# A fused attention and gated-convolution kernel: the last batch's gate products and the previous batch's output tiles move in between the last transform stages

## The chip, the cores and the metric

The kernel runs on one core of one Trainium2 chip. The metric is the device time of one execution in microseconds. The time before the change is the median of three runs.

## The reference

Two layers stand behind each other. The first is attention with a sparse mask (8 global keys and a causal window of 96 keys) and a bias by distance, over 4 batches, 8 heads, 768 positions and head size 64. The second is a gated long convolution over the sequence:

```python
x = attn_out.transpose(0, 2, 1, 3).reshape(B, S, H * D)     # (4, 768, 512)
proj = x @ w_proj                                            # (4, 768, 1536)
x1, x2, x3 = proj[..., :D], proj[..., D:2 * D], proj[..., 2 * D:]
X2 = np.fft.rfft(x2, n=S, axis=1)
Hf = np.fft.rfft(filter_fft, n=S, axis=0)[None]
x2_conv = np.fft.irfft(X2 * Hf, n=S, axis=1)
y = x1 * x2_conv * x3
out = y @ w_out                                              # (4, 768, 512)
```

The product `x1 * x3` is called the gate below, since it does not depend on the convolution.

## The kernel before, in words

The kernel does not issue its work as it is written down. Each method records operations in a `Plan`, with the keys that each reads and writes and a guessed cost. `Plan.schedule` then lists them greedily: of all operations that could start, it takes the one with the earliest start by its model, and among those within 0.03 us of each other the one with the smallest key. The key is the place of the operation's batch in time (`batch`, in periods of 40) plus `bias`. PSUM has 8 banks, each taken by one group of matmuls until it has been copied out, and the list scheduler hands them out. The result is a fixed order for each engine: TensorE (PE), VectorE (DVE), ScalarE (ACT), GpSimd (POOL) and the DMA queue of SyncE (SP). On the chip every engine works through its own list in order and waits where a semaphore tells it to.

Where the model leaves TensorE idle for long enough, `Plan.fill` writes extra matmuls on a tile of zeros into a spare bank (`busy`, line 356, tile `idle`). Their result is never read.

For each of four batches there are two parts, and the attention of batch b+1 is scheduled beside the convolution of batch b:

- `attention(b)`: transposes of q and k (line 608), scores (633), exp on ACT (645), masking on DVE (653, 656), values (677, 682), normalising on DVE (696, 697, tile `xn`), transposes of the result (712) into `xT`. This runs in three column groups c = 0, 1, 2. After c = 1 and c = 2 come the gates of one half of the sequence each: for each of four 128-column blocks j, `gate` runs two groups of four matmuls with 384 columns (739), scales the one by ACT into `x1` (364) and multiplies the other by it on DVE into `g` (747). At the end the butterfly makes `xa` and `xb` from the two sequence halves of `xT` (724, 726).
- `conv(b)`: six projection groups of four matmuls (line 783 before, 786 after) into `ab`; six forward transforms of three matmuls (595) into `X`; the products with the filter's spectrum on DVE (`spectra`, 852 to 863 before, 867 to 878 after); eight inverse transforms of three matmuls (803 before, 806 after) into `eo`; then on DVE the sum and the difference of `eo` give the two halves of `y` (812 before, 844 after), and each is multiplied by `g` (815 before, 847 after); last six output groups of four matmuls (826) are scaled by ACT into `ot` (364) and stored by a DMA of 256 KB from SP (834).

When the last batch's convolution begins, no attention is left to go beside it.

Of the kernel before, what the change touches and what calls it, by code (L numbers as in the profile page):

```python
# [29 lines left out]
def dve(n, rate=1, psum=False):  # L30
    return 0.068 + (0.005 if psum else 0.0) + n / rate / 960.0


def pe(*cols):
    return sum(n / 2400.0 + 0.0025 for n in cols)
# [242 lines left out]
class Fused:  # L278
# [472 lines left out]
    def attention(self, b):  # L751
        self.g.batch = (self.PERIOD * (b - 1 + self.SHIFT), self.PERIOD * self.LONG)
        for c in range(3):
            new = ([0, 1, 2], [3, 4], [5])[c]
            for t in new:
                self.transposes("q", t, self.qn[:, t], P * t)
            for t in self.GRP[c]:
                self.transposes("k", t, self.kn[:, t], P * t)
            for i in range(4):
                self.scores(i, c)  # L760
            for i in range(4):
                self.values(i, c, b % 2)
                if i % 2:
                    self.transpose_x(i // 2, c)
            if c:
                for j in range(4):
                    self.gate(b, j, c - 1)
        for j in range(2):
            self.butterfly(j)


    def conv(self, b):
        nc, g, DM, S = self.nc, self.g, self.DM, self.S
        h, last = S // 2, b == self.B - 1
        g.batch = (self.PERIOD * b, self.PERIOD)
        X, y, w = self.X, self.y, self.w
        for i, (src, key) in enumerate(((self.xa, "xa"), (self.xb, "xb"))):
            for t in range(3):
                bk = g.bank()

                def proj(_, src=src, t=t, bk=bk):
                    for c in range(4):
                        nc.tensor.matmul(bk.f32(), src[:, c, P * t:P * t + P], w[:, c, DM:2 * DM],  # L783
                                         start=(c == 0), stop=(c == 3))
                g.op("P", pe(*[512] * 4), proj, acq=[bk], r=[(key, 0), (key, 1)] + [
                    ("w", n) for n in range(4, 8)], name="proj")
                g.op("AV", self.evac(512), lambda e, i=i, t=t, bk=bk: self.copy(
                    e, self.ab[i][:, t, :], bk.f32()), use=[bk], w=[("ab", i, t)],
                    name="ab")
            if i == 0:  # L790
                self.spectra(b, (0, 1))
        self.spectra(b, (2, 3))
        self.spectra(b, (4, 5))
        for jp in range(2):
            eo, ke = self.eo[jp], ("eo", jp)
            for jj in range(2):
                for par, slots in ((0, (0, 1, 4)), (1, (2, 3, 5))):
                    bk = g.bank()
                    cs = slice(P * (2 * jp + jj), P * (2 * jp + jj) + P)

                    def turn(_, bk=bk, cs=cs, slots=slots):
                        for s in slots:
                            nc.tensor.matmul(bk.f32()[:, 0:h], X[:, s, cs], self.inv[:, s, :],  # L803
                                             start=(s == slots[0]), stop=(s == slots[-1]))
                    g.op("P", pe(h, h, h), turn, acq=[bk], r=[("X", s) for s in slots] + [("inv", s) for s in slots], name="inv")
                    g.op("AV", self.evac(h), lambda e, eo=eo, jj=jj, par=par, bk=bk: self.copy(
                        e, eo[:, jj, par], bk.f32()[:, 0:h]), use=[bk], w=[ke + (jj, par)], name="eo")
            yv = y[:, 2 * jp:2 * jp + 2].rearrange("p j (s n) -> p j s n", s=2)
            rs = [ke + (jj, par) for jj in range(2) for par in range(2)]
            gt = self.gt[b % 2]  # L810
            for half, fn in ((0, nc.vector.tensor_add), (1, nc.vector.tensor_sub)):
                g.op("V", dve(2 * h, 2), lambda _, fn=fn, yv=yv, eo=eo, half=half: fn(
                    yv[:, :, half], eo[:, :, 0], eo[:, :, 1]), r=rs, w=[("y", jp, half)], name="half")
                js = slice(2 * jp, 2 * jp + 2)
                g.op("V", dve(2 * h, 2), lambda _, js=js, half=half, gt=gt: nc.vector.tensor_mul(
                    y[:, js, h * half:h * half + h], y[:, js, h * half:h * half + h],
                    gt[:, js, h * half:h * half + h]),
                    r=[("y", jp, half)] + [("g", b % 2, j, half) for j in (2 * jp, 2 * jp + 1)],
                    w=[("y", jp, half)], name="y*g")
        osc = 1.0 / (S * H_SCALE * X1_SCALE)  # L820
        for t in range(6):
            bk = g.bank()

            def project(_, t=t, bk=bk):
                for c in range(4):
                    nc.tensor.matmul(bk.f32(), y[:, c, P * t:P * t + P], self.wo[:, c, :],  # L826
                                     start=(c == 0), stop=(c == 3))
            g.op("P", pe(*[512] * 4), project, acq=[bk], r=[("y", 0, t // 3), ("y", 1, t // 3), "wo"],
                 name="out")
            o = self.outs % 6  # L830
            self.outs += 1
            g.op("AV", self.evac(512), lambda e, o=o, bk=bk: self.times(e, self.ot[o], bk.f32(), osc),
                 use=[bk], w=[("ot", o)], name="ot")
            g.op("S", 0.5, lambda _, o=o, t=t, b=b: nc.sync.dma_start(
                self.out[b, P * t:P * t + P, :], self.ot[o]), r=[("ot", o)], nbytes=(128, 2048))

    def spectra(self, b, pair):
        nc, g, X = self.nc, self.g, self.X
        n = pair[0] // 2
        for s in pair:  # L840
            bk = g.bank()
            self.forward(s, self.ab, lambda i: [("ab", i, t) for t in range(3)], bk)
            g.op("AV", self.evac(512), lambda e, s=s, bk=bk: self.copy(e, X[:, s], bk.f32()),
                 use=[bk], w=[("X", s)], name="X")
        xs = X[:, pair[0]:pair[0] + 2]
        k = self.turn2 % 2
        self.turn2 += 1
        p1, p2 = self.p1[k], self.p2[k]
        hk = [("h", s) for s in pair] if n < 2 else [
            ("h", s, i, d) for s in pair for i in (1, 2) for d in (0, 64)]  # L850
        rs = [("X", s) for s in pair] + hk
        g.op("V", dve(1024, 2), lambda _: nc.vector.tensor_mul(p1, xs, self.h1[:, pair[0]:pair[0] + 2]),  # L852
             r=rs, w=[("p1", k)], name="prod")
        g.op("V", dve(1024, 2), lambda _: nc.vector.tensor_mul(p2, xs, self.h2[:, pair[0]:pair[0] + 2]),
             r=rs, w=[("p2", k)], name="prod")

        def sums(_):
            if n < 2:
                nc.vector.tensor_add(xs[:, 0], p1[:, 0], p2[:, 1])
                nc.vector.tensor_add(xs[:, 1], p1[:, 1], p2[:, 0])  # L860
            else:
                nc.vector.tensor_add(xs[0:64], p1[0:64], p2[64:P])
                nc.vector.tensor_add(xs[64:P], p1[64:P], p2[0:64])
        g.op("V", 2 * dve(512 if n < 2 else 1024, 2), sums, r=[("p1", k), ("p2", k)],
             w=[("X", s) for s in pair], name="sums")
# [96 lines left out]
```

## Time and profile before

| | |
|---|---|
| median of 3 runs | 207.98 us (206.68 to 208.18) |
| profiled execution, first to last instruction | 204.3 us |
| PE busy | 191.8 us (94%), 1688 matmuls, of them 58 on the tile of zeros |
| DVE busy | 152.2 us (75%) |
| ACT busy | 149.4 us (73%) |
| POOL busy | 75.5 us (37%), all of it in the first part of the span |

The page gives the span of the profiled execution and no separate time for it. The runs' median lies 3.7 us above that span; what is around the span is the start and the end of the program. A busy PE in this page includes the matmuls on zeros, so 94% is not a measure of useful work.

### The profile page before, as it was taken

How to read it: one execution, taken by the hardware profiler on the slowest of the kernel's cores; microseconds unless marked ns; L12 is line 12 of the kernel's file. 1: busy time of each engine (PE TensorE's matmuls, PEld its weight loads, DVE VectorE, ACT ScalarE, POOL GpSimd, SP SyncE). 2: the span in 40 equal slices, each digit the busy share in tenths (PEclk: the TensorE clock that was granted, in tenths of full speed). 3: DMA queues.
4: the chain of work that ended last, by engine and by line, in shares of the span. 5: the costliest groups of instructions: out<-in, count | busy, mean ns of one | idle time of the engine just before them, and what ended most of it. 6: DMA issues, size and time to landing. Idle time of an engine off the chain costs nothing.

```text
span 204.3 us, 4516 instructions
## 1 busy us (share of the span) xinstructions
PE 191.8 (94%) x1688; PEld 111.9 (55%) x1688; DVE 152.2 (75%) x382; ACT 149.4 (73%) x303; POOL 75.5 (37%) x96
## 2 busy tenths in 40 slices
PE   7993799999998899999999999999999999999992
PEld 2571565765545575754556577546555755444540
DVE  5983699993899999891499999529988995048520
ACT  3879997384999974685888678579985855682742
POOL 8969972897989994570001000000000000000000
PEclk9998599999999999999999999999999999999999
DMA  6999999999999999999404000250000002500025
GB/s 133 192 161 130 158 200 198 154 157 138 168 160 151 154 160 151 55 138 187 175 0 29 0 0 5 103 205 3 2 3 0 3 0 103 205 0 3 0 103 207
DMA packets 90933, 20.90 MB, mean 102 GB/s; under 512 B 83776, under 2 KB 87840, under 8 KB 90912
## 3 DMA queue, kind: packets, MB, share of 16 engines
q0 software_dynamic: 80912, 12.52, 91.3%
q1 hardware_dynamic: 10000, 8.10, 12.7%
q8 instruction: 13, 0.21, 0.4%
q14 instruction: 8, 0.07, 0.1%
HBM read 26.61 MB, written 6.29 MB: 161 GB/s over the span
## 4 chain that ended last, share of the span: by engine, by line
PE 82%; ACT 11%; DVE 4%; issue 2%; ACTq 0%
PE bank L739 20%; PE bank L826 10%; PE bank L783 9%; PE bank L803 8%; PE bank L356 7%; PE bank L595 6%; PE bank L608 5%; ACT E L645 5%; PE bank L633 4%; PE bank L677 4%; PE bank L712 3%; PE bank L682 3%; ACT h L364 2%; ACT mask L551 1%; DVE E L653 1%
## 5 line engine op out<-in xcount | busy, mean ns | idle before, releaser
L739 PE MATMUL bank<-xT,w 128*128 128x384 f16 x256 | 43.9, 326 | 0.0
L645 ACT ACTIVATE E<-bank 128x432 f16<-128x432 f32 x96 | 42.8, 565 | 0.9 <-PE bank L633 0.7
L739 PEld LDWEIGHTS <-w 128*128 128x128 f16 x256 | 24.8, 98 | 17.1
L376 POOL DMA_DIRECT2D kn<-in_k_dram x28 | 25.0, 907 | 23.1 <-PE bank L608 17.8
L364 ACT ACTIVATE x<-bank 128x384 f16<-128x384 f32 x31 | 15.7, 506 | 16.3 <-PE bank L739 14.5
L376 POOL DMA_DIRECT2D vn<-in_v_dram x28 | 25.1, 921 | 5.6 <-PE bank L682 4.8
L656 DVE TENSOR_TENSOR E<-E,mask 128x864 f16<-128x864 f16 x32 | 18.8, 601 | 7.2 <-ACT E L645 7.1
L697 DVE TENSOR_TENSOR xn<-bank,rc 128x256 f16<-128x256 f32 (+1 forms) x48 | 22.5, 469 | 1.7
L826 PE MATMUL bank<-wo,y 128*128 128x512 f16 x96 | 22.4, 379 | 0.0
L364 ACT ACTIVATE ot<-bank 128x512 f32<-128x512 f32 x24 | 14.3, 597 | 10.8 <-PE bank L826 10.8
L747 DVE TENSOR_TENSOR g<-bank,x 128x384 f16<-128x384 f32 x32 | 17.5, 551 | 6.2 <-PE bank L739 5.8
L360 ACT CAST eo<-bank 128x384 f16<-128x384 f32 x29 | 13.7, 490 | 10.7 <-PE bank L803 10.6
L677 PE MATMUL bank<-vn,E 128*128 128x65 f16 x224 | 18.7, 197 | 0.4
L803 PE MATMUL bank<-inv,X 128*128 128x384 f16 x96 | 18.9, 326 | 0.1
L356 PE MATMUL bank<-idle 128*128 128x512 f16 x58 | 17.5, 436 | 1.2 <-DVE warm L424 1.2
L677 PEld LDWEIGHTS <-E 128*128 128x128 f16 x224 | 15.4, 99 | 5.6 <-DVE E L656 1.3
L682 PE MATMUL bank<-vn,E 128*128 128x65 f16 x192 | 18.2, 195 | 0.0
L595 PE MATMUL bank<-ab,fwd 128*128 128x512 f16 x72 | 18.1, 379 | 0.0
L376 POOL DMA_DIRECT2D qn<-in_q_dram x18 | 16.0, 910 | 2.6 <-PE bank L783 1.1
L633 PE MATMUL bank<-QT,KT 64*128 64x216 f16 (+2 forms) x224 | 15.8, 248 | 0.9 <-DVE inv L360 0.2
L608 PE MATMUL bank<-ident,kn 128*128 128x128 f16 x112 | 11.1, 235 | 5.3 <-ACT E L645 4.2
L852 DVE TENSOR_TENSOR p<-X,h 128x1024 f16<-128x1024 f16 x12 | 8.2, 686 | 10.3 <-ACT X L360 10.2
(103 smaller groups left out, 334.0 us busy)
## 6 DMA issues: line engine op xcount, KB each, us to landing
out_dram<-ot SPq DMA_DIRECT2D x24, 256.0 KB
kn<-in_k_dram POOLq DMA_DIRECT2D x24, 128.0 KB, 5.8
vn<-in_v_dram POOLq DMA_DIRECT2D x24, 128.0 KB, 6.6
qn<-in_q_dram POOLq DMA_DIRECT2D x18, 128.0 KB, 7.6
ot<-in_q_dram SPq DMA_DIRECT2D x6, 256.0 KB
w<-in_moe_w_proj_dram POOLq DMA_DIRECT2D x4, 256.0 KB, 6.3
g<-in_moe_filter_fft_dram POOLq DMA_DIRECT2D x1, 768.0 KB, 12.6
w<-in_moe_w_proj_dram POOLq DMA_DIRECT2D x1, 512.0 KB, 9.1
```

The source lines that it names most:

```text
L356: self.nc.tensor.matmul(b.f32(), self.idle[:, 0:P], self.idle, start=True, stop=True)
L364: self.nc.scalar.mul(out, in_, c)
L376: return self.g.op(eng, 0.57 + 0.00035 * nbytes[0] if eng == "G" else 0.5, lambda _: e.dma_start(dst, src), w=w, r=r, nbytes=nbytes, name= ...
L595: self.nc.tensor.matmul(b.f32(), self.fwd[:, kt, s, :], src[i][:, kt, :], start=(kt == 0), stop=(kt == 2))
L633: nc.tensor.matmul(bs[hh].f32()[:, off:off + w], self.KT[hs, hp, P * m:P * m + P], self.QT[hs, hp, KL * m:KL * m + w], start=(off == 0), s ...
L645: g.op("A", act(432), lambda _, hh=hh: nc.scalar.activation(eo[:, hh], bs[hh].f32()[:, 0:432].rearrange("p (m w) -> p m w", m=2), Act.Exp, ...
L677: nc.tensor.matmul(o[:, hh, i], ef[:, at:at + P], vt[:, t, 2 * hp + hh, :], start=first, stop=(t == 0), skip_group_check=True)
L682: nc.tensor.matmul(o[:, hh, i], ef[:, at:at + P], vt[:, t - 1, 2 * hp + hh, :], start=False, stop=True, skip_group_check=True)
L697: nc.vector.tensor_mul(xn[:, ts[0]:ts[0] + nt].rearrange("p t h d -> p h t d"), o[:, :, :, 0:D], r.to_broadcast([P, 2, nt, D]))
L739: nc.tensor.matmul(bk.f32()[:, 0:h], self.w[:, c, o + P * j:o + P * j + P], self.xT[:, c, h * s:h * s + h], start=(c == 0), stop=(c == 3))
L803: nc.tensor.matmul(bk.f32()[:, 0:h], X[:, s, cs], self.inv[:, s, :], start=(s == slots[0]), stop=(s == slots[-1]))
L826: nc.tensor.matmul(bk.f32(), y[:, c, P * t:P * t + P], self.wo[:, c, :], start=(c == 0), stop=(c == 3))
```

## The change

Three things are changed, all of them for the end of the program alone.

1. `attention(3)` gives its gates a bias of 160 (half 0) and 200 (half 1), so that their key comes behind everything else, that of the last convolution included. They are taken only when nothing else can start.
2. `conv(2)` gives its output tiles a bias of 80 for the same purpose.
3. `conv(3)` does not write the two DVE operations for each half of `y` behind the inverse transforms of a column pair, but behind all of them: first half 0 for both pairs, then the output tiles 0 to 2, then half 1. The bias of 4 holds for half 1 and the fourth output tile.

```diff
             if c:
+                last = b == self.B - 1
                 for j in range(4):
+                    self.g.bias = 3.0 * self.PERIOD + self.PERIOD * c if last else 0.0
                     self.gate(b, j, c - 1)
+                self.g.bias = 0.0
...
-            yv = y[:, 2 * jp:2 * jp + 2].rearrange("p j (s n) -> p j s n", s=2)
-            rs = [ke + (jj, par) for jj in range(2) for par in range(2)]
-            gt = self.gt[b % 2]
-            for half, fn in ((0, nc.vector.tensor_add), (1, nc.vector.tensor_sub)):
...
+            if not last:
+                for half in range(2):
+                    self.gated(b, jp, half)
         osc = 1.0 / (S * H_SCALE * X1_SCALE)
         for t in range(6):
+            if last and t % 3 == 0:
+                g.bias = 4.0 * (t // 3)
+                for jp in range(2):
+                    self.gated(b, jp, t // 3)
+            if b == self.B - 2:
+                g.bias = 2.0 * self.PERIOD
             bk = g.bank()
...
+            g.bias = 0.0
+
+    def gated(self, b, jp, half):
+        nc, g, y, h = self.nc, self.g, self.y, self.S // 2
+        eo, gt = self.eo[jp], self.gt[b % 2]
+        js = slice(2 * jp, 2 * jp + 2)
+        hs = slice(h * half, h * half + h)
+        fn = nc.vector.tensor_sub if half else nc.vector.tensor_add
+        g.op("V", dve(2 * h, 2), lambda _: fn(y[:, js, hs], eo[:, :, 0], eo[:, :, 1]),
+             r=[("eo", jp, jj, par) for jj in range(2) for par in range(2)],
+             w=[("y", jp, half)], name="half")
+        g.op("V", dve(2 * h, 2), lambda _: nc.vector.tensor_mul(y[:, js, hs], y[:, js, hs],
+                                                                gt[:, js, hs]),
+             r=[("y", jp, half)] + [("g", b % 2, j, half) for j in (2 * jp, 2 * jp + 1)],
+             w=[("y", jp, half)], name="y*g")
```

What the scheduler makes of it is seen in the order on the engines. Up to the first gate of the last batch both programs have the same order on every engine; all that follows differs.

The first place is ACT in the last batch's attention, where the first four of the gates stood ahead of the exps of column group 2 (`E`). `x_95` to `x_98` are the four buffers of `x1`. Before:

```order
L364 ACTIVATE x_95<-bank_118 128x384
L364 ACTIVATE x_96<-bank_122 128x384
L364 ACTIVATE x_97<-bank_123 128x384
L364 ACTIVATE x_98<-bank_120 128x384
L645 ACTIVATE E_67<-bank_118 128x2x216
L645 ACTIVATE E_67<-bank_124 128x2x216
```

And the same place of the changed program:

```order
L364 ACTIVATE x_95<-bank_118 128x384
L645 ACTIVATE E_67<-bank_124 128x2x216
L645 ACTIVATE E_67<-bank_122 128x2x216
L645 ACTIVATE E_68<-bank_119 128x2x216
L645 ACTIVATE E_68<-bank_123 128x2x216
L645 ACTIVATE E_69<-bank_125 128x2x216
L645 ACTIVATE E_69<-bank_120 128x2x216
L645 ACTIVATE E_70<-bank_121 128x2x216
L645 ACTIVATE E_70<-bank_118 128x2x216
L364 ACTIVATE x_96<-bank_122 128x384
L360 CAST eo_93<-bank_123 128x384
```

The exps moved ahead of all gates but one. On PE the same is seen as follows: before, 32 gate matmuls stand in a row ahead of the scores; now 4 stand there, then the 24 of the scores, then 12 more gate matmuls, and the inverse transforms and values of this stage after them. At its end PE has 20 gate matmuls in both programs; before, 12 more follow between the output tiles of batch 2, and 16 matmuls of the last four of these tiles behind them; now two output tiles (8 matmuls) follow, and then the projections of the last batch.

The second place is DVE at the end of that stage, where batch 2's `y` (with its gates `g_85`) and the last batch's `xa` and `xb` are made. Before:

```order
L812 TENSOR_TENSOR y<-eo_93 128x2x384 x2
L815 TENSOR_TENSOR y<-y,g_85 128x2x384 x2
L812 TENSOR_TENSOR y<-eo_94 128x2x384 x2
L815 TENSOR_TENSOR y<-y,g_85 128x2x384
L747 TENSOR_TENSOR g_86<-bank_121,x_95 128x384
L815 TENSOR_TENSOR y<-y,g_85 128x2x384
L724 TENSOR_TENSOR xa<-xT 128x768
L747 TENSOR_TENSOR g_86<-bank_122,x_96 128x384
L726 TENSOR_TENSOR xb<-xT 128x768
```

And now:

```order
L844 TENSOR_TENSOR y<-eo_93 128x2x384 x2
L847 TENSOR_TENSOR y<-y,g_85 128x2x384 x2
L724 TENSOR_TENSOR xa<-xT 128x768
L844 TENSOR_TENSOR y<-eo_94 128x2x384 x2
L847 TENSOR_TENSOR y<-y,g_85 128x2x384 x2
L726 TENSOR_TENSOR xb<-xT 128x768
```

The gate products between them are gone from this place; those whose matmuls still stand here come behind the butterfly.

The third place is the last convolution, between the forward and the inverse transforms. ACT before, where the four copies of `X` end and the copies of the inverse transforms (`eo`) begin:

```order
L360 CAST X<-bank_125 128x512
L360 CAST X<-bank_120 128x512
L360 CAST X<-bank_123 128x512
L360 CAST X<-bank_121 128x512
L360 CAST eo_93<-bank_124 128x384
```

ACT now:

```order
L360 CAST X<-bank_124 128x512
L364 ACTIVATE ot_101<-bank_120 128x512
L360 CAST X<-bank_121 128x512
L360 CAST X<-bank_123 128x512
L360 CAST X<-bank_119 128x512
L364 ACTIVATE ot_102<-bank_125 128x512
L364 ACTIVATE ot_103<-bank_122 128x512
L364 ACTIVATE ot_104<-bank_118 128x512
L364 ACTIVATE x_96<-bank_120 128x384
L364 ACTIVATE x_97<-bank_123 128x384
L360 CAST eo_93<-bank_119 128x384
```

DVE from there to the end of the program, where the last `y` is made, in the changed program:

```order
L878 TENSOR_TENSOR X<-p_90,p_91 64x1024
L747 TENSOR_TENSOR g_86<-bank_124,x_95 128x384
L747 TENSOR_TENSOR g_86<-bank_121,x_96 128x384
L844 TENSOR_TENSOR y<-eo_93 128x2x384 x2
L847 TENSOR_TENSOR y<-y,g_86 128x2x384 x2
L844 TENSOR_TENSOR y<-eo_94 128x2x384 x2
L847 TENSOR_TENSOR y<-y,g_86 128x2x384
L747 TENSOR_TENSOR g_86<-bank_119,x_97 128x384
L747 TENSOR_TENSOR g_86<-bank_122,x_98 128x384
L847 TENSOR_TENSOR y<-y,g_86 128x2x384
```

Before, the same eight operations on `y` stood there in the same sequence, with no gate product ahead of them or between them. On PE the change is this: one of batch 2's output tiles (4 matmuls) now stands ahead of the last three forward transforms; three more (12 matmuls) and 16 gate matmuls stand where 20 matmuls on zeros stood, between the forward and the inverse transforms; the last 12 gate matmuls and one matmul on zeros stand where 10 on zeros stood, between the inverse transforms and the final output tiles. The 5 on zeros between the transposes of the last batch's attention are gone, so that 35 of them became 1. The final output tiles are run in the order 0, 1, 2, 4, 5, 3.

More of the change, by code (lines that the diff above doesn't have):

```diff
@@ L807, in conv @@
                         e, eo[:, jj, par], bk.f32()[:, 0:h]), use=[bk], w=[ke + (jj, par)], name="eo")
-            yv = y[:, 2 * jp:2 * jp + 2].rearrange("p j (s n) -> p j s n", s=2)
-            rs = [ke + (jj, par) for jj in range(2) for par in range(2)]
-            gt = self.gt[b % 2]
-            for half, fn in ((0, nc.vector.tensor_add), (1, nc.vector.tensor_sub)):
[L812 to L819, printed above, removed]
+            if not last:
+                for half in range(2):
+                    self.gated(b, jp, half)
         osc = 1.0 / (S * H_SCALE * X1_SCALE)
         for t in range(6):
+            if last and t % 3 == 0:
[4 more added lines that the diff above has]
+                g.bias = 2.0 * self.PERIOD
             bk = g.bank()
```

## Prediction

> **What bounds the kernel now.** I began with the page's first two lines.
>
> ```profile
> span 204.3 us, 4516 instructions
> PE 191.8 (94%) x1688; PEld 111.9 (55%) x1688; DVE 152.2 (75%) x382; ACT 149.4 (73%) x303; POOL 75.5 (37%) x96
> ```
>
> PE looks full, but matmuls on zeros count in it. Which of its pieces set the end is told by the chain that ended last, in order of time (start, length, what), from the first gate of the last batch on:
>
> ```profile
> 151.57 5.21 PE bank L739 x32
> 156.78 0.48 PE bank L633 x12
> ...
> 163.16 0.49 PE bank L803 x3
> 163.65 0.43 PE bank L356 x2
> 164.08 0.34 PE bank L712 x6
> 164.41 0.65 PE bank L356 x3
> 165.06 3.25 PE bank L739 x20
> ...
> 171.99 3.45 PE bank L826 x16
> 175.44 4.32 PE bank L783 x20
> 179.75 1.29 PE bank L595 x6
> 181.05 0.86 PE bank L783 x4
> 181.91 2.59 PE bank L595 x12
> 184.50 4.32 PE bank L356 x20
> ...
> 192.98 2.16 PE bank L356 x10
> 195.14 5.19 PE bank L826 x24
> ```
>
> The chain stays on PE to the end, and line 356 in it is work on zeros: 2, 3, 20 and 10 matmuls, 0.43 + 0.65 + 4.32 + 2.16 = 7.56 us. In these places PE really waits for others, the two long ones in the last convolution, where no attention is left to fill them. I call stage A what runs from 151.57 to 175.44, where the last projections (line 783) begin, and stage B from there to 195.14, where the last output tiles begin. What follows 195.14 is the same work before and after: 24 matmuls, the last scaling, the last store.
>
> Prices from these rows: a 512-column matmul costs 3.45 / 16 = 0.216 us, on zeros too (4.32 / 20); a 384-column one costs 5.21 / 32 = 0.163.
>
> **The change on PE.** Stage A loses 28 of 64 gate matmuls (28 x 0.163 = 4.56 us), 16 of 24 output matmuls (3.45) and all five on zeros (1.08): 9.09 us. Stage B takes the same 4.56 + 3.45 in, loses 30 on zeros (6.48) and gains one (0.22): it grows by 1.75 us. If PE waits nowhere anew, the program ends 9.09 - 1.75 = 7.34 us earlier, which is the 34 matmuls on zeros at 0.216. The rest is to find the new waits.
>
> **Stage A: what comes late next.** These rows of the timeline (start, length, engine, line, operation) carry it:
>
> ```profile
> 151.44 0.71 ACT L360 COPY KT<-bank 128x480 f16<-128x480 f16 x1
> ...
> 154.43 0.69 DVE L862 TENSOR_TENSOR X<-p,p 64x1024 f16<-64x1024 f16 x1
> 155.13 0.69 DVE L863 TENSOR_TENSOR X<-p,p 64x1024 f16<-64x1024 f16 x1
> 155.85 1.59 DVE L747 TENSOR_TENSOR g<-bank,x 128x384 f16<-128x384 f32 x3
> ...
> 157.10 3.49 ACT L645 ACTIVATE E<-bank 128x432 f16<-128x432 f32 x8 [0.39 <-PE bank L633]
> 158.36 1.18 DVE L656 TENSOR_TENSOR E<-E,mask 128x864 f16<-128x864 f16 x2
> ...
> 162.57 0.56 DVE L697 TENSOR_TENSOR xn<-bank,rc 128x384 f16<-128x384 f32 x1
> 163.26 0.56 DVE L697 TENSOR_TENSOR xn<-bank,rc 128x384 f16<-128x384 f32 x1
> 163.74 1.01 DVE L812 TENSOR_TENSOR y<-eo 128x768 f16<-128x768 f16 x2
> ...
> 169.82 0.55 DVE L726 TENSOR_TENSOR xb<-xT 128x768 f16<-128x768 f16 x1
> ```
>
> After four gate matmuls (to 152.2) PE goes to the scores, which need the last copy of `KT`, done at 152.15: a wait of 0.1 to 0.2 us that 28 gate matmuls covered. The 24 scores take two times 0.48 and end near 153.4. The exps start about 0.39 after the first of them, as now, near 152.8 instead of 157.10, and run at 3.49 / 8 = 0.44. The next gate group needs the bank of the first exp, free near 153.3: 0.1 us. Three gate groups (1.95) end near 155.4; the inverse transforms need the sums of line 863. Without the gate product of 0.55 ahead of them these end near 155.2, so there is no wait.
>
> DVE then runs masks (0.59 each) from 155.3, each behind its pair of exps, to 157.6, one gate product to 158.2, and four times reciprocal and normalising at the spacing of 163.26 - 162.57 = 0.69: the second ends near 159.6, the fourth near 161.0. PE gets to the first transposes of `xn` near 159.3 and waits 0.4 us, where matmuls on zeros would no longer cover it; to the second ones without a wait. The 20 gate matmuls end near 165.2. DVE makes `y` of batch 2 in eight operations at about 0.47 from 161.0, with one butterfly step in between: its first half is done near 164.8, ahead of PE by 0.4. Two output tiles end near 167; `xa` is complete near 166.2, again ahead. New waits: 0.15 + 0.1 + 0.4, and 0.25 for hand-overs that I can't list, 0.9 us in all. Stage A gains 9.09 - 0.9 = 8.2 us.
>
> Bounds: nothing waits anew (9.09), or DVE comes no earlier than it does now. Then the butterfly ends at 169.82 + 0.55 = 170.37 as before, the projections start near 170.5 instead of 175.44, and stage A gains 4.9.
>
> ```profile
> 151.40:164.90 13.50, 13.50 (x147) 8.64 (x146) 12.83 (x29) 9.68 (x22) 0.00 (x0) 1.00 0.01 2
> 164.90:175.28 10.38, 10.38 (x58) 5.48 (x57) 6.49 (x14) 5.13 (x10) 0.00 (x0) 1.00 0.20 78
> ```
>
> These windows (length, busy us of PE, weight loads, DVE, ACT, POOL, then clock, DMA) show why DVE is the engine to watch: it is busy 12.83 of 13.50 us in the first one. But three gate products (0.53 each) and two copies of `eo` that DVE did there go to later places or to ACT, which has 3.8 us idle. I stay near the upper end.
>
> **Stage B: does the moved work fit?** The chain here is PE, ACT, DVE, PE. I measure from the start of the projections.
>
> ```profile
> 182.60 2.53 ACT L360 CAST X<-bank 128x512 f16<-128x512 f32 x4
> 184.51 0.69 DVE L852 TENSOR_TENSOR p<-X,h 128x1024 f16<-128x1024 f16 x1 [0.72 <-ACT X L360]
> ...
> 188.41 0.68 DVE L863 TENSOR_TENSOR X<-p,p 64x1024 f16<-64x1024 f16 x1
> 189.60 3.95 ACT L360 CAST eo<-bank 128x384 f16<-128x384 f32 x8 [4.48 <-PE bank L803]
> 191.63 1.03 DVE L812 TENSOR_TENSOR y<-eo 128x768 f16<-128x768 f16 x2 [2.54 <-ACT eo L360]
> ...
> 194.53 1.02 DVE L815 TENSOR_TENSOR y<-y,g 128x768 f16<-128x768 f16 x2
> ```
>
> One output tile ahead of the last forward transforms delays them by 4 x 0.216 = 0.86 us, and with them `X` and the products. DVE's run from 184.51 to 189.09 (4.58) then ends 0.86 later against the projections. Behind the forward transforms PE now has 12 x 0.216 + 16 x 0.163 = 5.20 us in place of 4.32, so it reaches the inverse transforms 0.86 + 0.88 = 1.74 later than now. PE is the later of the two by 0.9, less the 0.1 to 0.3 that PE now waits there for the sums: the moved work covers DVE's run completely and overshoots a little. The price of the overshoot is what the sum above has as stage B's growth.
>
> From there the copies of `eo` (8 at 0.49) and DVE's `y` follow the inverse transforms as now. PE has 12 gate matmuls and one on zeros, 2.17 us, where 2.16 on zeros stood. Ahead of the first `y` DVE has two gate products (1.1 us), which it does in the wait of 2.54 that the row at 191.63 shows. The other two stand between the halves of `y*g`: half 1 comes 0.95 later, while output tiles 0 to 2, which read half 0, run for 12 x 0.216 = 2.6 us. That cover holds; gone, it would cost 0.95 once. Of the held-back stores the last goes out about 9 us ahead of the first final one. I cost them at nothing. **The third edit, half by half, I cost at nothing as well:** the DVE order of the eight operations on `y` is what it was, because the list scheduler takes the sums as soon as `eo` is there.
>
> Stage B grows by 1.75 less the short wait ahead of the inverse transforms, about 0.1: 1.65.
>
> **Sum.** 8.2 - 1.65 = 6.5 us; I take 6.4 earlier: a span of 197.9 instead of 204.3. The median of 207.98 lies 3.7 above that span; nothing around the span changes, so 207.98 - 6.4 = **201.6 us**.
>
> **Two rules of the skill.** The Trainium skill, "TensorE: Matmul & The Clock Gate", section "Back-to-back issue gap", gives about 131 ns per matmul with 512 columns in a sustained stream with weight loads. By it 34 matmuls would be worth 4.45 us, and with 0.9 of waits the gain would be near 3.6. The trace disagrees: 24 such pairs of weight load and matmul take 5.19 us in the chain's last row, 216 ns each, and so this has no chance of its own.
>
> The other speaks against the change. The clock that PE was granted, by windows:
>
> ```profile
> 15.00:20.00 5.00, 2.13 (x26) 1.18 (x24) 2.21 (x7) 4.99 (x7) 5.00 (x7) 0.94 1.93 128
> 20.00:25.00 5.00, 3.13 (x33) 2.26 (x33) 2.67 (x8) 5.00 (x13) 5.00 (x7) 0.50 1.78 156
> 25.00:30.00 5.00, 4.70 (x71) 3.10 (x69) 4.89 (x17) 4.71 (x12) 3.85 (x6) 0.88 1.36 197
> ```
>
> Where PE idled for 2.87 of 5 us, the clock then fell to half and stayed there for some 6 us. The same page, "What's actually happening" with its table of two states, says that an idle window of about 3.4 us closes the gate; "A second HAM failure mode" says that short idles between groups of matmuls can do it too. The trace bears out the first; of the second it shows nothing.
>
> **Rivals.** (1) DVE bounds stage A, and it gets no earlier: the projections start near 170.5, the gain is 4.9 - 1.65 = 3.3, the time 204.7. For it speaks DVE's 95% in the first window; against it that it has about 2.7 us less to do before the butterfly. Chance 0.10. (2) The clock falls once, since short waits are now bare. As in the three windows this costs 0.06 x 5 + 0.50 x 5 + 0.12 x 5 = 3.4 us: 205.0. Against it: the longest idle stretch in my walk is 0.4 us. Chance 0.04. (3) Slower: stage B grows and stage A gives nothing, because the scores and exps that are now early fill DVE's and PE's queues ahead of what the projections need, and these still start at 175.44. The price is the overshoot of 1.65: 209.6. It decides from the point at which stage A gains under 1.65. The butterfly, done at 170.37, 5 us ahead of the projections, speaks against it. Chance 0.02. (4) The change does not do what it says: for the third edit I take that as given; for the first two the order excludes it, so this rival, with 207.98, has no chance of its own.
>
> **How the numbers follow.** My forecast, new waits of 0 to 2 us on PE and so a gain of 5.4 to 7.4, has 0.84: 200.6 to 202.6 by this median. Runs before spread from 206.68 to 208.18, so 0.4 on the lower side is added; the upper side takes in half of rival 1's way. Range 200.2 to 204.2. About 1% (2.1 us) is what a measurement here can tell from no change, so faster means below 205.9: forecast, rivals 1 and 2 in the main, 0.96; same 0.03; slower 0.01.
>
> **What would show it.** In the changed profile about 1654 matmuls and PE busy near 185; the first of 24 matmuls of line 786 in the last batch near 167.3; no wait of PE over 0.6 us after 150; exps of group 2 from 152.8; the inverse transforms held by PE's own queue and no longer by the sums; the final 24 output matmuls near 188.7. It would be wrong if DVE idles in stage A behind ACT or PE, if the clock falls below 0.9 after 150, or if the final output tiles wait in the middle for half 1.

## The result, and the profile after

The changed kernel takes 200.19 us in the median of four runs (199.12 to 201.03), against 207.82 for the kernel before in the runs beside it. The ratio is 0.964, with a 95% interval of 0.958 to 0.970: 7.6 us faster.

The first two lines of the changed kernel's page:

```profile
span 198.0 us, 4444 instructions
PE 185.1 (93%) x1654; PEld 109.7 (55%) x1654; DVE 151.0 (76%) x380; ACT 150.3 (76%) x305; POOL 75.7 (38%) x96
```

There are 34 matmuls fewer, and PE's share hardly moves: by this line alone the two kernels look alike. The chain that ended last, in order of time, from the first gate of the last batch on, shows what happened:

```profile
152.55 0.67 PE bank L739 x4
...
153.63 0.54 ACT E L645
154.17 0.04 issue
154.21 2.11 PE bank L739 x12
156.32 0.97 PE bank L806 x6
...
160.36 0.51 PE bank L712 x6
160.87 0.98 PE bank L806 x6
161.84 0.41 PE bank L712 x6
162.26 0.49 PE bank L806 x3
162.75 3.25 PE bank L739 x20
166.00 1.73 PE bank L826 x8
167.72 4.32 PE bank L786 x20
172.04 1.29 PE bank L595 x6
173.33 0.86 PE bank L786 x4
174.20 0.65 PE bank L595 x3
174.84 0.86 PE bank L826 x4
175.71 1.94 PE bank L595 x9
177.65 2.59 PE bank L826 x12
180.24 2.60 PE bank L739 x16
182.84 3.90 PE bank L806 x24
186.74 1.95 PE bank L739 x12
188.69 0.22 PE bank L356
188.91 5.19 PE bank L826 x24
```

From 162.75 to the last output tile PE goes from one useful group to the next without a wait; of line 356 one matmul is left in this part. Stage A, to the first projection, now takes 167.72 - 152.55 = 15.17 us (23.87 before), stage B 188.91 - 167.72 = 21.19 (19.70 before). Together that is 36.36 instead of 43.57: 7.21 us shorter. I call this the end section; what follows it is 9.1 us in both.

The span fell by only 6.3 us, because in this execution the first gate of the last batch started 0.98 us later than in the one profiled before, though the order of instructions up to there is the same. Experiment 9 returns to this.

The windows of the two stages (length, busy us of PE, weight loads, DVE, ACT and POOL, then clock and DMA) show how close the second engine is:

```profile
152.55:167.72 15.17, 15.09 (x154) 9.58 (x152) 14.88 (x33) 11.51 (x26) 0.00 (x0) 1.00 0.00 1
167.72:188.91 21.19, 21.19 (x113) 10.87 (x111) 12.35 (x25) 15.24 (x28) 0.00 (x0) 1.00 0.20 75
```

In stage A DVE is busy for 14.88 of 15.17 us, nearly as much as PE. Which of the two sets the end there can't be read from busy shares; experiments 5 and 6 ask for it. The granted clock is 1.00 in both stages.

### The profile page after: what moved, and what is told of

Its sections match the earlier page's. It is cut to its first block, busy times and chain, and to the rows that moved or that the text cites. A ratio compares the mean times of both kernels' runs of the same rounds, so it can differ in the third digit from the quotient of the medians.

```text
span 198.0 us, 4444 instructions
## 1 busy us (share of the span) xinstructions
PE 185.1 (93%) x1654; PEld 109.7 (55%) x1654; DVE 151.0 (76%) x380; ACT 150.3 (76%) x305; POOL 75.7 (38%) x96
## 4 chain that ended last, share of the span: by engine, by line
PE 72%; DMA 10%; POOL 9%; DVE 4%; issue 2%; ACT 1%; POOLq 0%; ACTq 0%
PE bank L739 19%; PE bank L786 11%; PE bank L826 10%; PE bank L595 8%; PE bank L806 8%; DMA kn<-in_k_dram 5%; DMA w<-in_moe_w_proj_dram 5%; PE bank L633 4%; PE bank L677 3%; POOL vn L376 3%; PE bank L608 3%; PE bank L712 3%; POOL kn L376 3%; PE bank L682 2%; POOL w L376 1%
## 5 line engine op out<-in xcount | busy, mean ns | idle before, releaser
L364 ACT ACTIVATE x<-bank 128x384 f16<-128x384 f32 x31 | 15.7, 508 | 15.4 <-PE bank L739 14.3
L360 ACT CAST eo<-bank 128x384 f16<-128x384 f32 x31 | 14.7, 487 | 7.2 <-PE bank L806 6.8
L677 PE MATMUL bank<-vn,E 128*128 128x65 f16 x224 | 19.6, 201 | 0.1
L677 PEld LDWEIGHTS <-E 128*128 128x128 f16 x224 | 16.3, 103 | 4.9 <-DVE E L656 1.3
L682 PE MATMUL bank<-vn,E 128*128 128x65 f16 x192 | 19.1, 199 | 0.0
L682 PEld LDWEIGHTS <-E 128*128 128x128 f16 x192 | 14.7, 101 | 1.2
L826 PEld LDWEIGHTS <-y 128*128 128x128 f16 x96 | 9.4, 98 | 10.5
```

Of the source, the lines that this page charges most:

```text
L364: self.nc.scalar.mul(out, in_, c)
L677: nc.tensor.matmul(o[:, hh, i], ef[:, at:at + P], vt[:, t, 2 * hp + hh, :], start=first, stop=(t == 0), skip_group_check=True)
L682: nc.tensor.matmul(o[:, hh, i], ef[:, at:at + P], vt[:, t - 1, 2 * hp + hh, :], start=False, stop=True, skip_group_check=True)
```

## The experiments

Two theories at first. **A:** PE's own list sets the end, and what is gained is the time of the matmuls on zeros that go, 0.216 us each. **B:** the gain comes because DVE loses gate products ahead of the butterfly; DVE sets the pace of the last attention. Since whole runs of one program vary by more than 1 us, the end section is compared beside the times.

**1. The gates alone.** The two edits on output tiles and halves are undone.

```diff
-            if b == self.B - 2:
-                g.bias = 2.0 * self.PERIOD
```

> Only the first edit: the last batch's gates are held back, batch 2's output tiles and the halves stay as before. 38 matmuls on zeros are left in the program (58 before, 24 in the full change). Theory A, PE's own list sets the end and only the matmuls on zeros that go are gained: 20 x 0.216 = 4.3 us less than before, ratio 0.979; from the first gate of the last batch to the first final output tile 43.6 - 4.3 = 39.3 us. Theory B, the gain comes because DVE gets its gate products and copies of eo out of the last attention and so reaches the butterfly sooner: nearly the whole gain of the full change, about 7.2 us, ratio 0.965.

Measured: 203.71 us, ratio 0.982 (0.978 to 0.987); end section 192.79 - 153.42 = 39.37 us. The chain of this kernel, its last convolution:

```profile
181.75 3.90 PE bank L739 x24
185.65 1.08 PE bank L356 x5
186.73 3.90 PE bank L806 x24
190.63 2.16 PE bank L356 x10
192.79 5.19 PE bank L819 x24
```

The section is 4.20 us shorter than before, for 20 matmuls on zeros fewer (0.21 each), as A said. DVE has lost the same gate products from the last attention as in the full change, and the rest of the gain is not there: B falls as the main cause.

**2. The output tiles alone.** The gates and the halves are undone.

```diff
-                    self.g.bias = 3.0 * self.PERIOD + self.PERIOD * c if last else 0.0
```

> Only the second edit: batch 2's output tiles are held back, the gates and the halves stay as before. 39 matmuls on zeros are left. Theory A: 19 x 0.216 = 4.1 us less than before, ratio 0.980. Theory B: these tiles cost DVE nothing, so nothing is gained in the last attention and the projections wait for the butterfly: within 1% of before.

Measured: 202.69 us, ratio 0.977 (0.973 to 0.982); end section 192.43 - 153.22 = 39.21 us, 4.36 shorter for 19 matmuls on zeros fewer. These tiles take nothing off DVE, and still nearly the same is gained. The projections start right behind the gates, which the chain of this kernel shows:

```profile
166.71 5.20 PE bank L739 x32
171.91 4.32 PE bank L783 x20
```

The two edits do not add up (4.20 + 4.36 = 8.56 against 7.21), since both fill the same idle time.

One sum gives all three sizes. The matmuls on zeros that went count 0.216 us each. To them comes the short wait ahead of the last inverse transforms, which took 0.33 + 0.10 + 3.74 = 4.17 us before and take 3.90 in all three kernels: 0.27. Where gates are held back, 0.39 of new waits in the attention are taken off; that figure is from the full change, whose stage A lost 9.09 us of work and became 8.70 shorter. Gates alone: 4.32 + 0.27 - 0.39 = 4.20, measured 4.20. Output tiles alone: 4.10 + 0.27 = 4.37, measured 4.36. Both: 7.34 + 0.27 - 0.39 = 7.22, measured 7.21.

**3. The halves alone.** Both biases are undone.

> Only the third edit: the last result by halves. The order of PE and DVE is that of before, only the last three copies of the output and their stores change places. Both theories: the same time as before within 0.3%.

Measured: 206.96 us, ratio 0.999 (0.996 to 1.002); end section 195.91 - 152.33 = 43.58 us, 43.57 before. On its own the third edit is worth nothing.

**4. Half of the gates.** Only column blocks 2 and 3 are held back.

```diff
-                    self.g.bias = 3.0 * self.PERIOD + self.PERIOD * c if last else 0.0
+                    self.g.bias = 3.0 * self.PERIOD + self.PERIOD * c if last and j >= 2 else 0.0
```

> The full change, but only the gates of column blocks 2 and 3 are held back, those of blocks 0 and 1 stay where they were. 30 matmuls on zeros are left, 6 more than in the full change and 28 fewer than before. Theory A: 28 x 0.216 = 6.0 us less than before, ratio 0.971, and 1.3 us more than the full change. Theory B: half of the gate products are back on DVE in the last attention (four at about 0.5 us), so 2 us more than the full change, unless DVE had that much room.

Measured: 201.03 us, ratio 0.970 (0.966 to 0.974); end section 190.19 - 152.13 = 38.06 us, 1.70 more than the full change, between the two expectations. Its chain shows both parts:

```profile
156.89 0.60 DVE E L656
157.49 0.47 DVE x L366
157.95 0.53 DVE E L656
...
188.69 1.51 PE bank L356 x7
```

Seven matmuls on zeros instead of one at the end are 1.29 us: A. The other 0.4 is a wait for masks on DVE, between which a scaling of `x1` has been put. So DVE is close behind PE, and a gate that is put back there can make it late.

**5 and 6. How much room DVE has.** The full change, and DVE repeats the first `xa` of the last batch once or four times; the results are the same.

```diff
+        again = 4 if self.last and j == 0 else 0
+
+        def total(_):
+            for _ in range(1 + again):
+                self.nc.vector.tensor_add(self.xa[:, hs], xT[:, hs, 0:h], xT[:, hs, h:])
```

> The full change, and DVE makes the first xa of the last batch twice (one more tensor_add of 0.47 us in the last attention, the order of everything else unchanged, the result the same). In the changed profile the first half of batch 2's y ends 0.4 us ahead of the output tiles that read it, and xa 0.7 us ahead of the projections. Theory A, DVE is just behind PE: under 0.1 us, the same time as the full change. Theory B, DVE sets the pace of the last attention: 0.47 us more.

> The full change, and DVE makes the first xa of the last batch five times (four more tensor_adds of 0.47 us, 1.88 us in all). Theory A: 1.88 less the room of 0.4 us, 1.4 to 1.5 us more than the full change, with a wait of PE for y of that length ahead of the first held output tile. Theory B: 1.9 us more.

Measured: with one more, 199.07 us and an end section of 188.51 - 152.15 = 36.36 us, exactly that of the full change. With four more, 201.78 us and 190.30 - 152.16 = 38.14 us. The chain of the second, where it leaves PE for DVE:

```profile
163.34 0.48 DVE xa L728
163.82 0.02 issue
163.84 0.57 DVE xa L728
164.41 0.02 issue
164.44 0.57 DVE xa L728
...
165.62 0.56 DVE xa L728
166.18 0.94 DVE y L849 x2
167.12 0.48 DVE y L852
167.60 0.05 issue
167.65 1.47 PE bank L831 x6
```

In this chain each repeat starts 0.02 us behind the end of the one before and takes 0.56 to 0.57 instead of 0.48, so four take 166.18 - 163.82 = 2.36 us and not the 1.88 that I had expected. The section grows by 1.78: DVE's room ahead of the held output tiles is 2.36 - 1.78 = 0.58 us. So PE sets the pace, but only just: with 0.6 us more work in this place DVE would, and from there on B is true.

**7. The zeros taken out of the kernel before.** The question is whether their time was only a wait.

```diff
-                if n > 0:
+                if n > 0 and o.batch[0] < 120.0:
```

> The kernel before without the 30 matmuls on zeros in the last convolution (the 28 earlier ones stay), so that PE stands idle there for 4.3 and 2.2 us. If these matmuls only fill a wait, and the clock holds: the same time as before. If the clock falls as it did between 15 and 25 us: the inverse transforms (3.9 us) and a part of the 24 final output matmuls run at half speed, 2 to 5 us more, with a granted clock near 0.5 to 0.9 after 185 us.

Measured: 208.51 us, ratio 1.007 (1.002 to 1.011), so 1.2 us more by the medians: little, but the interval lies above 1. From the first gate to the end of the last output matmul it is 202.61 - 151.92 = 50.69 us, against 200.33 - 151.57 = 48.76 before: 1.9 more. The windows of this kernel, with the granted clock third from the end:

```profile
184.20:189.60 5.40, 0.98 (x7) 0.33 (x5) 4.54 (x8) 1.17 (x2) 0.00 (x0) 0.78 0.00 0
189.60:194.56 4.96, 4.96 (x18) 2.40 (x19) 1.00 (x3) 2.40 (x5) 0.00 (x0) 0.55 0.01 3
194.56:197.68 3.12, 1.39 (x9) 0.58 (x7) 2.52 (x7) 1.44 (x3) 0.00 (x0) 1.00 0.00 0
```

PE idles behind the last forward transforms (busy 0.98 of 5.40 us), the clock falls to 0.55 on average in the next window, and 16 inverse transforms take 4.96 us, 0.31 each against 3.90 / 24 = 0.16. The final output matmuls no longer suffer: the clock is back at 1.00 ahead of them, so the cost stays just under the 2 to 5 us expected. The zeros took up a wait that was there anyway, and they did more than fill it: they kept the clock up. In the last convolution of the changed kernel one of them is left, and the clock stays at 1.00: useful matmuls do the same.

**8. Fewer held tiles.** Only the last four of batch 2's output tiles get the bias.

> The full change, but of batch 2's output tiles only the last four are held back by the bias; the first two are taken at their own key. 24 matmuls on zeros are left, as in the full change. Theory A: the same time as the full change within 0.3%, wherever the tiles stand. A theory in which the tile ahead of the last forward transforms costs its 0.86 us would give a different time only if that tile had moved.

Measured: 199.58 us, end section 188.76 - 152.41 = 36.35 us. The scheduler gave PE the order of the full change, so this is a repeat of it and tells no theory apart.

**9 and 10. The part ahead of the end section.** The full change again, and the same with five matmuls on zeros where PE waits for keys near 66 us.

```diff
+        n = 5 if what == "k" and t == 2 and self.now == 2 else 0
+
         def turn(_):
+            self.busy(n, b)
```

> The full change once more, beside the next kernel on the same chip. In the profiles so far the stretch from the first gate of the last batch to the first final output tile hardly varies for one program, while what lies ahead of it, the same order of instructions in all of them, ends between 151.6 and 153.4 us. If the granted clock in the middle of the program (a fall to 0.5 for some 3 us near 70 us, in some executions) is the cause, executions with a higher mean clock are the shorter ones: spans near 197.3 at 0.98, up to 199.3 at 0.964.

> The full change, and five matmuls on zeros (1.08 us) ahead of the key transposes of batch 2 that wait there 0.9 us for a DMA near 66 us; they write the bank that these transposes then take. Theory C, the short idles of PE from 64 to 71 us let the clock fall in some executions: these zeros hold it, no fall near 70 us, 0.5 to 1 us less than the full change in the median, and less spread. Theory D, the fall has another cause: the same time as the full change, or up to 0.2 us more for the matmuls that don't fit into the wait.

Measured: 199.51 us, ratio 0.963 (0.959 to 0.968), and 199.19 us, ratio 0.962 (0.958 to 0.967). The end sections are 189.73 - 153.39 = 36.34 and 188.27 - 151.92 = 36.35 us. Windows of the full change's second profile around the place:

```profile
66.00:67.00 1.00, 0.49 (x8) 0.25 (x5) 1.00 (x4) 0.96 (x3) 1.00 (x3) 1.00 2.43 155
...
71.00:72.00 1.00, 0.84 (x18) 0.67 (x15) 0.93 (x5) 1.00 (x4) 0.86 (x2) 0.77 2.43 155
72.00:73.00 1.00, 1.00 (x21) 1.00 (x19) 0.96 (x4) 1.00 (x3) 1.00 (x2) 0.50 2.43 155
```

And with the five zeros:

```profile
66.00:67.00 1.00, 0.85 (x5) 0.39 (x4) 1.00 (x4) 0.96 (x3) 0.96 (x2) 1.00 2.42 154
...
71.00:72.00 1.00, 0.92 (x22) 0.77 (x22) 0.93 (x5) 1.00 (x3) 1.00 (x3) 1.00 2.42 154
72.00:73.00 1.00, 1.00 (x31) 0.99 (x28) 0.93 (x5) 1.00 (x3) 1.00 (x3) 1.00 2.43 155
```

In the first the clock is at half between 72 and 73 us; in the second it holds. Of six executions each, three had a mean clock of 0.98 or more without the zeros, and five with them. Their spans at 0.98 and above lie at 196.9 to 197.8 us without the zeros and 197.2 to 197.6 with them; the others reach 198.7 and 199.1 (one execution without the zeros has 197.4 at 0.970). That favours theory C, and the kept profiles say more for it. In the window from 66 to 69 us PE was busy for 1.98 us or less in eight of the twelve profiles (1.49 to 1.98), and in each of them the clock fell between 67 and 75 us (in that of experiment 7 already inside the window). In the four others it was busy for 2.00 us or more (2.00, 2.06 and 2.12, and 2.59 with the five zeros), and the clock stayed at 1.00. The program does not decide it: the profile of the kernel before shows no fall, and that of experiment 7, with the same order on every engine up to the last inverse transforms, shows one. The margin is small and was found after the fact, so it is no threshold.

What this is worth in time is not settled. The medians differ by 0.3 us and the intervals overlap. Of the eleven profiles with one order up to the end section, the three without a fall reach it at 151.57, 152.15 and 152.33 us, the eight with one at 151.92 to 153.42: the fall explains a part of the spread at most.

## Why the prediction was right

The mechanism was right: PE's list sets the end, and useful work takes the place of work on zeros. The sizes were all on the cautious side. The forecast was 201.6 us with a gain of 5.4 to 7.4, and the measured 200.19 with a gain of 7.6 lies beyond that, at the lower end of the whole range (200.2). Two repeats of the same program have medians of 199.58 and 199.51 us, beside 207.31 and 207.03 for the kernel before, gains of 7.7 and 7.5 us: the gain is steady, and the range had little to spare on this side.

- **That the zeros on PE are what is gained: shown.** 34 fewer shortened the end section by 7.21 us, 0.212 each; the single edits have nearly the same price (0.210 and 0.229), and the sum under experiment 2 accounts for the differences. The Trainium skill, "TensorE: Matmul & The Clock Gate", section "Back-to-back issue gap", has 131 ns for such a pair in a stream; the runs do not agree with it.
- **New waits in stage A: over-estimated.** The term was 0.9 us; the stage gained 23.87 - 15.17 = 8.70 of the 9.09 possible, so it measured 0.39. The chain shows where. Against the prices of the prediction the twelve gate matmuls behind the scores take 0.16 more, a value matmul that waits for a mask 0.14 more (0.17 instead of 0.03; this wait was not listed), and the transposes of `xn` 0.24 more (0.51 and 0.41 instead of 0.34 each), where 0.4 was forecast; the scores start almost without a wait. That is nearly 0.6 in all. But the inverse transforms lost two waits of 0.1 that they had before (0.59 and 1.08 for three and six; now six take 0.97 and three 0.49), which the sum had not counted, and so about 0.4 is left. The walk itself held: the exps begin 1.08 us after the first gate (1.2 forecast), the first projection 15.17 after it (15.7).
- **DVE close behind, but hidden: shown.** Its room was put at 0.4 us ahead of the output tiles and is 0.58. The signs named for a failure did not appear: DVE idles for 0.3 us of stage A, the clock is 1.00 in both stages, and the final output tiles run without a pause.
- **Growth of stage B: 1.65 forecast, 1.49 measured.** The inverse transforms took 4.17 us before and take 3.90 now, so the wait for the sums that went is 0.27 and not the 0.1 in the sum.
- **Half 1 of `y` behind two gate products: hidden, as said.** The 24 final matmuls take 5.19 us in both.
- **Rival 1 (DVE bounds stage A)** had the first projection 18.9 us after the first gate; it came after 15.17. The single edits and experiment 5 speak against it too. **Rival 2 (the clock)** did not touch the end section, but its mechanism is real: experiment 7 shows it there with bare waits, for 1.9 us. That short idles can bring it about had no row in the prediction. In the profile of experiment 9 the clock fell though PE's longest idle stretch from 60 to 72 us was 0.5 us. The Trainium skill, "TensorE: Matmul & The Clock Gate", section "A second HAM failure mode", tells of a clock that swings because PE idles briefly and often between groups of matmuls; these windows fit it. **Rival 3** would have needed stage A to stand still.
- **From the span to the median: a step with two errors.** I took 3.7 us as what lies around the span, and as unchanged. The first hardly mattered: the runs show 2.1 (206.45 us beside a span of 204.3), and the profiled execution was a short one. The second was wrong: the time around the span is 2.1 to 2.2 us in all 37 executions of the kernel before whose span is on record, and 1.7 to 1.8 in the 14 of the full change (199.78 beside 198.0), so 0.35 less. Over the programs run here it goes with the number of DVE instructions: 1.7 to 1.9 with 380 or 381, 2.1 to 2.2 with 382 or 384. Why is open; no run was made for it.

So the median fell by 7.6 us: 7.21 from the end section, 0.35 from around the span, and the small rest from the part ahead. That the rest is so small is luck, since that part varies by more than 1 us from run to run. The forecast was 1.4 us too high: 0.5 from the waits, 0.16 from the growth, 0.15 because 6.55 was taken as 6.4, 0.35 from around the span, 0.16 because the kernel before has 207.82 and not 207.98 in the runs beside it, and the rest from the part ahead.

## What to carry to other kernels

When an engine is full, look at what it is full of: filler work on the path shows where an engine waits, and its sum is about the most that moving useful work there can bring. Before taking filler out, look at the clock: here it kept the clock up. Move work that nobody needs soon (last products, last outputs) into the tail where no next batch is left, and count the new waits where it stood, and the old ones that go. Look at the engine that comes next: here DVE has 0.6 us of room left, so taking more than that off PE in the last attention should bring nothing unless DVE is relieved too (no run shows this). Compare one section between two events of the trace when the rest of the program varies by more than the effect sought.

## What the runs showed of the hardware that was not expected

The granted clock can fall with no long idle: in the changed kernel's first profile it stood at 0.57 on average between 69 and 73 us after PE had been busy 1.77 of the 3 us from 66 to 69, with no single wait over 0.9 us.

```profile
66.00:69.00 3.00, 1.77 (x25) 1.07 (x24) 3.00 (x9) 2.94 (x7) 2.94 (x5) 1.00 2.42 156
69.00:73.00 4.00, 3.88 (x56) 3.35 (x56) 3.75 (x11) 4.00 (x11) 4.00 (x5) 0.57 2.47 154
```

The start of the end section varied between 151.57 and 153.42 us over eleven profiles with one order of instructions up to there, while the end section of the full change was 36.36, 36.35 and 36.34 us in three profiles.
